# A long convolution by transforms beside a sliding-window attention: the second transform level moved to 64x64 tiles

## The chip, the cores and the metric

The kernel runs on one core of a Trainium2 chip. A core has a matrix engine (TensorE, PE in the profile, with PEld for its weight loads), three engines for elementwise work (VectorE or DVE, ScalarE or ACT, GpSimd or POOL), an engine that mostly issues transfers (SyncE or SP) and 16 DMA engines. PE writes into PSUM; DVE or ACT copies the results from there into SBUF (an eviction). The metric is the device time of one execution in microseconds.

## What is computed

Two independent parts, whose results stand side by side in the output rows (2048 rows of 576 + 576 bf16 numbers).

```
# A: attention over 8 positions, 2 apart, 32 heads of 18
q, k, v = split(x @ wqkv)                 # x: 2048 x 576
logits  = q[s] . k[s - 2*w] * 18**-0.5    # w = 0..7, masked below 0
o       = softmax(logits) . v[s - 2*w]
a       = o @ wo                          # 576 x 576

# B: short convolution, gate, long convolution, gate
k_shift = sum over t < 4 of k[s - t] * shift_k[:, t]
kv      = k_shift * v
y       = causal convolution of kv with ssm_k (2048 taps per channel)   # by rfft of length 4096
b       = q * (y + kv * ssm_D)
```

## The kernel before

**The long convolution** is done by a transform in two levels, in bf16 matmuls. Time is split as s = 16a + t, with a on the 128 partitions and t = 0..15. The first level (`s1_part`; steps `sx` for the signal kv, `kp` for the taps, which `kt` transposes first) multiplies by a 128x128 table for the real and one for the imaginary part and gives, for each first frequency f of 128, 32 rows: 16 t by real and imaginary. The results go to scratch arrays in DRAM (`Dk`, `Dx`) with f and rows exchanged, so that the second level can have the rows on the partitions. There f is split as (l, h). Step `kl` or `xl` number i loads one block (`w_load`), step `ks` or `xs` transforms it (`k_spec`, `x_spec`, helper `s2`), `gp` multiplies the two spectra (`g_prod`), `gi` transforms back (`g_inv`) and writes to the scratch `Dy`. `yl` loads it turned back (`y_load`), `ys` does the inverse of the first level and multiplies by q (`y_step`), and the result leaves for DRAM. There are 8 blocks i, each step of the second level runs twice per block (.0 and .1).

Before, a block is one half of the 576 channels (i // 4) and 8 of the 32 values of h (i % 4); the 128 partitions hold 32 rows by 4 values of l. `s2` uses tables of 128x64 with zeros between different l, one for the real and one for the imaginary part, and two matmuls side by side fill a PSUM tile. X and K then have real and imaginary part in separate columns; `g_prod` makes all four products of them; `g_inv` adds them up in four matmuls per tile of 64 x 128, with a third table that is the negative of the first (`ia_minus`, steps `im`). A scratch row is 288 numbers, 576 bytes. A `yl` needs the four blocks of its own half of the channels.

**The attention**: `xt` transposes x, `qk`, `qt` and `v` project it, `lm` multiplies q by a shifted k on DVE, `lb` sums over heads on PE, `sm` is the softmax for one half hv of the positions, `pm` multiplies the weights with shifted v on DVE, `ps` sums over the window by identity matmuls on 64x64 tiles, `po` is the output projection (72 matmuls of 32x128 tiles, 288 columns), and `pz` is a `po` with the last two `ps` inside. `po.0.*` needs all nine `ps.0.*`.

**The order.** One list, `ORDER`, written out by hand or by a planner outside the kernel, gives all steps. Each engine runs its own instructions in this order, and the order holds for the queues of SP (almost all transfers) and POOL (the Dy writes and a small halo of v) as well; semaphores make an instruction wait for data or for a free buffer, and all behind it on its engine wait too. A step may carry marks: `a` or `b` names one of two PSUM pools (two tiles each), `s` or `v` says that ACT or DVE does its eviction. Without a mark `evac` uses ACT (L102, DVE is L104), and the copies of `xt` and `kt` use DVE (L359). Buffers come from small rings: four slots for loaded blocks, two each for K, X and the products.

Of the kernel before, what the change touches and what calls it, by code (L numbers as in the profile page):

```python
# [18 lines left out]
lx.2.1 lx.2.0 lx.1.1 lx.1.0 tj lx.0.1 t0 lx.0.0 tv lwt t2 lwq.0.1 lwq.1.1 wm.11:b xt.2.2:bs xt.2.0:bs xt.1.0:as sk.2:b  # L19
xt.1.2:bs xt.1.1:as t3 xt.2.1:b sk.1:a xt.0.0:bs qk.0.1.1:a lx.3.0 lx.3.1 lk.1 tw sk.0:av qk.1.1.2:b xt.0.2:a xt.0.1:b  # L20
xt.3.1:a t4 lk.0 wt cv.0.0 cv.0.4 lkn.4 xt.3.0:as lkn.0 xt.3.2:bs qk.1.1.1:b lkn.1 qk.0.1.3:b cv.1.1 lkn.2 qt.1:b
cv.1.4 qt.3:a lkn.3 lwq.0.0 qt.2:b lv.0 cv.0.1 lk.2 lwq.1.0 lwv cv.1.0 kt.7:b kt.1:a cv.0.3 kp.7.0:a cv.0.2 cv.1.3
kp.7.1:b cv.0.5 cv.1.5 kp.7.2:b kt.2:as qk.0.0.0:a t5 lv.1 cv.0.6 kp.1.0:b cv.1.2 lk.3 kp.1.1:a cv.0.7 qk.1.0.2:b
kp.1.2:a cv.1.6 cv.1.7 kt.0:bs ib ia.5 kp.2.0:a qk.0.1.2:b ld cv.2.1 cv.2.4 kp.2.1:a kp.2.2:a qt.0:b lv.3 sx.0.0:b
qk.0.0.2:a sx.0.1:b cv.2.3 sx.0.2:a qk.0.0.1:b kp.0.0:a kp.0.1:a qk.0.0.3:b lv.2 ia.2 kp.0.2:a sx.1.0:b sx.1.1:a
qk.0.1.0:b sx.1.2:b qk.1.0.0:a t1 cv.3.3 cv.3.4 ia.3 cv.2.5 sx.2.0:b cv.3.1 sx.2.1:a cv.2.0 cv.2.2 cv.3.5 qk.1.1.3:b
cv.2.6 sx.2.2:av kt.3:a sx.3.0:b sx.3.1:bv kt.5:as sx.3.2:a cv.3.0 qk.1.1.0:b kp.3.0:a cv.3.2 kp.3.1:b qk.1.0.3:a
kp.3.2:a ia.7 cv.3.6 cv.2.7 kp.5.0:bv ia.1 kp.5.1:b kt.4:as kp.5.2:b kt.6:as ia.0 cv.3.7 qk.1.0.1:b lm.0.1 sx.4.0:a
sx.4.1:b sx.4.2:a v.4:b lm.0.2 v.0:b lm.6.2 lm.0.0 lb.0:a sx.6.0:a sx.6.1:b lm.6.0 sx.6.2:b lm.6.1 kp.4.0:a ia.4
lb.6:a kp.4.1:b kp.4.2:a ia.6 lm.7.0 v.8:b lm.7.1 sx.7.0:b sx.7.1:a sx.7.2:a lb.7:b sx.5.0:b sx.5.1:a sx.5.2:a lm.4.0  # L30
lm.1.0 v.7:b kp.6.0:a kp.6.1:b kp.6.2:a kl.3 lm.1.1 lm.4.2 lb.1:b xl.3 im.0 xl.2 xl.5 v.2:a lm.2.0 v.5:a im.1 lm.4.1
lm.2.2 lb.4:b v.1:b lm.2.1 lm.5.0 lb.2:b ks.3.0:a v.3:b vh.0 xs.3.0:a lm.5.1 xs.3.1:b lb.5:a kl.5 ks.3.1:b lm.3.0 kl.6
vz xs.5.0:a lm.3.1 lb.3:b xs.5.1:a vh.1 ks.5.0:b gp.3.0 sm.0.0 ks.5.1:a sm.1.0 ql.1 sm.0.1 ql.3 sm.1.1 sm.0.2 sm.0.3
sm.1.2 sm.0.4 kl.2 gp.3.1 sm.1.3 xs.2.0:bv v.6:a xl.6 sm.0.5:a lwo.3 gi.3.0:a lwo.0 sm.0.6 xs.2.1:a kl.0 gp.5.0 pm.0.1
vh.2 ks.6.0:b ks.6.1:a gi.5.0:b gp.5.1 gi.3.1:a ps.0.1:b xs.6.0:a xs.6.1:b ks.2.0:a pm.0.0 gp.6.0 pm.0.3 sm.1.4
ps.0.0:b xl.0 lwo.2 gi.5.1:a xl.1 sm.1.5:b pm.0.7 gp.2.0 gi.6.0:a gp.6.1 ks.2.1:b ps.0.3:a kl.1 sm.1.6 xs.0.0:b
gi.6.1:a pm.0.5 ps.0.7:b gp.2.1 pm.0.6 ks.0.0:a pm.1.0 ks.0.1:b xl.7 gi.2.0:a ps.0.5:b gi.2.1:a gp.0.0 xs.1.0:b
ks.1.0:a ps.0.6:b gp.1.0 xs.1.1:a gi.0.0:b xs.0.1:a ql.0 pm.1.3 ps.1.0:b ks.1.1:a kl.7 ps.1.3:b gp.0.1 ql.2 xs.7.0:a
pm.0.8 gi.1.0:b gp.1.1 kl.4 xl.4 gi.0.1:a pm.0.4 ks.7.0:b gi.1.1:a ps.0.8:b ks.4.0:b lwo.1 ks.4.1:a pm.0.2 xs.4.0:b
# [9 lines left out]
def kernel(  # L49
# [50 lines left out]
    def evac(dst, src, scale=None, on="s"):  # L100
# [8 lines left out]
    Dx = dram.tile([2, 32, 128, HD], BF16, name="Dx")  # L109
    Dy = dram.tile([2, 32, 128, HD], BF16, name="Dy")  # L110
    VT = 528

    def by_f1(Dd, dh, r0, n):
        return Dd[dh].rearrange("r f d -> f r d")[:, r0:r0 + n, :]
# [105 lines left out]
    mk = r2  # L220
# [484 lines left out]
```

## Time and profile before

Three runs took 208.24, 208.3 and 210.26 us, median 208.3. The profiled execution took 208.09 us; its span, from first to last instruction of the program, is 206.1 us, so 2 us lie around it. TensorE's granted clock was 1.0 until the last slices (0.995 in the mean).

| stretch (us) | what runs | PE | DVE | ACT | DMA share |
|---|---|---|---|---|---|
| 0 to 20 | loads, tables, transposes of x | 17.0 of 20 | 15.7 | 14.1 | 0.95 |
| 20 to 60 | first level, projections, short convolution | 39.4 of 40 | 37.5 | 34.2 | 0.86 |
| 60 to 105 | first level, logits | 43.7 of 45 | 44.7 | 37.5 | 0.68 |
| 105 to 120 | second level begins, softmax | 13.2 of 15 | 14.2 | 14.1 | 0.94 |
| 120 to 169.5 | second level, weights times v | 46.0 of 49.5 | 48.3 | 48.9 | 0.87 |
| 169.5 to 201.3 | output projection, last inverse level | 31.2 of 31.8 | 21.0 | 14.2 | 0.93 |
| 201.3 to the end | last evictions and writes | 0 of 4.8 | 0 | 1.2 | 0.60 |

Busy times are those of the engine in that stretch. PE's come from pipelined matmuls, so a full PE need not be at its peak. DMA moved 51.5 MB in 54,398 packets, most of them of 576 bytes.

### The profile page before, as it was taken

What the parts mean: (1) busy time and instruction counts of PE and PEld (TensorE: products, weight loads), DVE (VectorE), ACT (ScalarE), POOL (GpSimd) and SP (SyncE); (2) the same over time, 40 slices, a digit from 0 to 9 for tenths busy, and PEclk for the clock granted to TensorE, in tenths of its full rate; (3) what the DMA queues carried; (4) which work ended last, traced back from release to release, by engine and by line L of the source; (5) the groups of instructions that cost most, each with busy time, mean ns of one, the idle gap of its engine ahead of it and who ended that gap; (6) DMA issues with size and microseconds to landing.
All of it is one profiled execution on the core that took longest, in us unless ns stands there. A gap on an engine that the chain in (4) does not pass through costs nothing.

```text
span 206.1 us, 6334 instructions
## 1 busy us (share of the span) xinstructions
PE 190.5 (92%) x2725; PEld 123.7 (60%) x2725; DVE 181.3 (88%) x160; ACT 164.1 (80%) x251; POOL 13.0 (6%) x39
## 2 busy tenths in 40 slices
PE   7699999999999999999998798899998999999990
PEld 2456465444465674556655575666666669876880
DVE  7877999997899999999999999999999989871740
ACT  2698788997879968897598999999999984804342
POOL 8300000000000000000210101111011011000000
PEclk9999999999999999999999999999999999999997
DMA  6999999789743874966958999987498598899995
GB/s 170 310 384 231 405 343 267 241 258 257 212 130 115 227 198 132 195 189 157 413 140 271 275 205 305 256 321 276 144 368 283 175 329 305 214 318 280 266 257 176
DMA packets 54398, 51.50 MB, mean 250 GB/s; under 512 B 6769, under 2 KB 48354, under 8 KB 54370
## 3 DMA queue, kind: packets, MB, share of 16 engines
q1 hardware_dynamic: 53120, 46.32, 77.1%
q0 software_dynamic: 1248, 4.77, 6.2%
q8 instruction: 21, 0.34, 0.7%
q14 instruction: 7, 0.06, 0.1%
q10 hardware_dynamic: 2, 0.00, 0.0%
HBM read 31.04 MB, written 18.87 MB: 242 GB/s over the span
## 4 chain that ended last, share of the span: by engine, by line
PE 56%; ACT 31%; issue 5%; DMA 2%; POOL 2%; DVE 2%; ACTq 1%; SPq 0%; DVEq 0%; POOLq 0%
ACT area L102 28%; PE psB L373 11%; PE psA L612 7%; PE psA L373 5%; PE psB L380 4%; PE psA L652 3%; PE psA L428 2%; PE psA L601 2%; DMA Dk<-area 2%; PE psB L612 2%; PE psA L380 2%; ACT area L528 2%; PE psB L428 2%; PE psB L601 2%; PE psB L578 2%
## 5 line engine op out<-in xcount | busy, mean ns | idle before, releaser
L102 ACT ACTIVATE area<-psA 128x576 bf16<-128x576 f32 (+6 forms) x119 | 86.5, 782 | 19.6 <-PE psB L612 9.1
L102 ACT ACTIVATE area<-psB 128x576 bf16<-128x576 f32 (+8 forms) x118 | 83.9, 749 | 12.4 <-PE psB L373 4.9
L590 DVE TENSOR_TENSOR area<-area,area 128x4096 bf16<-128x4096 bf16 x18 | 40.7, 2283 | 0.0
L489 DVE TENSOR_TENSOR area<-area 128x4096 bf16<-128x4096 bf16 x16 | 35.7, 2285 | 0.3 <-PE psB L506 0.2
L373 PEld LDWEIGHTS <-area 128*128 128x128 bf16 x160 | 15.5, 98 | 17.1 <-issue 0.4
L373 PE MATMUL psB<-area,area 128*128 128x512 bf16 x110 | 25.4, 379 | 0.1
L457 DVE TENSOR_TENSOR area<-area,area 128x2304 bf16<-128x2304 bf16 x16 | 21.0, 1351 | 2.6 <-PE psB L428 1.9
L565 DVE TENSOR_TENSOR area<-area 128x2304 bf16<-128x2304 bf16 x16 | 21.6, 1353 | 1.2 <-ACT area L102 1.1
L543 PEld LDWEIGHTS <-W 128*64 128x64 bf16 x256 | 13.7, 108 | 11.3 <-issue 11.0
L612 PE MATMUL psA<-area,area 32*128 32x288 bf16 x288 | 19.4, 282 | 0.6 <-ACT area L102 0.3
L612 PE MATMUL psB<-area,area 32*128 32x288 bf16 x288 | 19.2, 282 | 0.0
L380 PEld LDWEIGHTS <-area 128*32 128x32 bf16 x360 | 15.6, 140 | 4.7 <-issue 1.4
L612 PEld LDWEIGHTS <-area 32*128 32x128 bf16 x576 | 16.1, 93 | 3.6 <-issue 1.6
L601 PEld LDWEIGHTS <-ident 64*64 64x64 bf16 x576 | 15.1, 107 | 3.5 <-issue 2.8
L578 PEld LDWEIGHTS <-IAt 64*128 64x128 bf16 x256 | 12.4, 94 | 6.4 <-issue 3.3
L451 DVE TENSOR_TENSOR area<-area,area 128x2304 bf16<-128x2304 bf16 x12 | 15.8, 1352 | 0.1
L543 PE MATMUL psA<-area,W 128*64 128x288 bf16 x136 | 13.3, 291 | 1.3 <-ACT area L102 0.3
L428 PEld LDWEIGHTS <-T 128*128 128x128 bf16 x96 | 8.7, 98 | 9.4 <-issue 2.8
L380 PE MATMUL psB<-area,area 128*32 128x512 bf16 x240 | 14.1, 382 | 0.2 <-ACT area L102 0.2
L428 PE MATMUL psA<-area,T 128*128 128x384 bf16 x54 | 13.1, 327 | 0.6 <-ACT area L102 0.4
L601 PE MATMUL psB<-area,ident 64*64 64x256 bf16 x384 | 12.6, 271 | 0.2
L543 PE MATMUL psB<-area,W 128*64 128x288 bf16 x120 | 11.4, 290 | 1.3 <-ACT area L102 0.9
(112 smaller groups left out, 212.2 us busy)
## 6 DMA issues: line engine op xcount, KB each, us to landing
Dk<-area SPq DMA_DIRECT2D x16, 288.0 KB, 3.5
Dx<-area SPq DMA_DIRECT2D x16, 288.0 KB, 3.0
area<-Dk SPq DMA_DIRECT2D x8, 576.0 KB, 4.9
area<-Dx SPq DMA_DIRECT2D x8, 576.0 KB, 6.7
Dy<-area POOLq DMA_DIRECT2D x8, 576.0 KB, 4.4
area<-Dy SPq DMA_DIRECT2D x8, 576.0 KB, 5.2
area<-in_A_wo_dram SPq DMA_DIRECT2D x4, 648.0 KB, 9.4
area<-in_A_x_dram SPq DMA_DIRECT2D x8, 288.0 KB, 5.5
```

The source lines that it names most:

```text
L102: nc.scalar.activation(dst, src, ACT.Copy, **({} if scale is None else {"scale": scale}))
L373: nc.tensor.matmul(ps[:, u, :], w[:, kb, cols[u]:cols[u] + 128], xT[:, j, kb], start=(kb == 0), stop=(kb == 4))
L380: nc.tensor.matmul(ps[32 * a:32 * a + 32, u, :], wv[:, kb, 2 * n + u:D:DH], xT[:, a, kb], start=(kb == 0), stop=(kb == 4), tile_position=( ...
L428: nc.tensor.matmul(ps[:, ri, 0:384], T1[:, ri, :], sf[:, 384 * ch:384 * ch + 384], start=True, stop=not extra)
L457: nc.vector.tensor_tensor(dst, kfull[:, 4 * c + 3 - j:4 * c + 7 - j, :], skb[:, j, :].unsqueeze(1).to_broadcast([128, 4, D]), ALU.mult)
L489: nc.vector.tensor_tensor(prr.get((n, h)), q2[h], k2[h][:, :, o0:o0 + S], ALU.mult)
L543: nc.tensor.matmul(ps[64 * hp:64 * hp + 64, im, 0:HD], W2[:, im, 8 * g + 2 * prl + hp].rearrange("p l f -> p (l f)"), Wt[:, 2 * prl + hp, ...
L565: nc.vector.tensor_tensor(Pv, Xv.unsqueeze(2).to_broadcast([128, 2, 2, 2 * HD]), Kv.unsqueeze(1).to_broadcast([128, 2, 2, 2 * HD]), ALU.mult)
L578: nc.tensor.matmul(ps[:, hp, 0:HD], IAt[r, tab, 4 * g + 2 * hv + u, :], Pp[(i, hv)][r, n, u, :], start=(n == 0), stop=(n == 3), tile_posit ...
L590: nc.vector.tensor_tensor(Pr.get((hv, p)), vv, Lt[:, :, 256 * hv:256 * hv + 256].unsqueeze(2).to_broadcast([128, W, 2, 256]), ALU.mult)
L601: nc.tensor.matmul(ps[64 * b:64 * b + 64, r, 0:256], ident[g, g], P[g, n, :, 128 * b:128 * b + 128], start=(n == 0), stop=(n == W - 1), ti ...
L612: nc.tensor.matmul(pss[e][:, b, 0:HD], Os[hv][g, d // 2, r, 128 * (d % 2):128 * (d % 2) + 128], wo4[g, d, d0:d1], start=(d == 0), stop=(d ...
```

## The change

The second level works on 64x64 tiles. A block is now 4 of the 32 values of h and all 576 channels; the partitions hold two halves a of f, each 32 rows by 2 values of l. Four matmuls of 64x64 fill a PSUM tile, one in each quarter of the array, and real and imaginary part lie on neighbouring partitions of the result. For the product each partition needs its own part of K and its neighbour's, so a new step `kz` (`k_swap`) copies K with odd and even partitions exchanged, by two transfers from SBUF to SBUF. `gp` makes the two products, `gi` adds them up in two rounds of four 64x64 matmuls instead of four rounds of two. The table for `gi` comes from a new array `Wp`, which the new step `tp` (`t_pairs`, three ACT copies) fills; `im` goes. Scratch rows are 576 numbers, 1152 bytes, so are the rows of q and of the output, except for half of the attention's. A `yl` now needs all eight blocks. One memset moves from `tv` to `ld`. K's ring gets an area of its own.

The list of steps is written anew from the first to the last: the order, the PSUM pools and the evicting engines are all different. The first convolution is now `cv.0.1` instead of `cv.0.0`; the blocks of the second level come as 3 5 1 4 7 0 2 6 instead of 3 5 6 2 0 1 7 4; two of the five `kt` copies that ACT made are now DVE's; the inverse first level `ys` starts behind the first four `po`, where two steps of it ran ahead of the first `po`.

```diff
-    Dk = dram.tile([2, 32, 128, HD], BF16, name="Dk")
+    Dk = dram.tile([2, 32, 64, D], BF16, name="Dk")
...
     def t_w2():
         nc.scalar.preload_act_table_set("natural_log_exp_and_others")
-        for i in range(2):
-            nc.vector.tensor_tensor(W2[:, i], C2[:, 32 * i:32 * i + 32].unsqueeze(2).to_broadcast([128, 32, 4, 16]),
-                                    lmask.unsqueeze(1).to_broadcast([128, 32, 4, 16]), ALU.mult)
+        nc.vector.tensor_tensor(W2.rearrange("p h (l f) -> p h l f", l=2), C2.unsqueeze(2).to_broadcast([128, 32, 2, 32]),
+                                lmask.unsqueeze(1).to_broadcast([128, 32, 2, 32]), ALU.mult)
+
+    def t_pairs(i):
+        dst = Wp[:, i].rearrange("p h (f j) -> p (h f) j", j=2)
+        src = W2[:].rearrange("p h (f i) -> p (h f) i", i=2)[:, :, i:i + 1]
+        if i:
+            evac(dst, src.to_broadcast([128, 1024, 2]))
+        else:
+            evac(dst[:, :, 0:1], src)
+            evac(dst[:, :, 1:2], src, scale=-1.0)
...
-    def s2(Wt, g, dst, h, scale):
-        for prl in (2 * h, 2 * h + 1):
+    def s2(Wt, i, dst, q, scale):
+        for d0, d1 in DCH:
             ps = psb()
-            for im in range(2):
-                for hp in range(2):
-                    nc.tensor.matmul(ps[64 * hp:64 * hp + 64, im, 0:HD],
-                                     W2[:, im, 8 * g + 2 * prl + hp].rearrange("p l f -> p (l f)"),
-                                     Wt[:, 2 * prl + hp, :], start=True, stop=True, tile_position=(0, 64 * hp))
-            evac(dst[:, :, prl, :], ps[:, :, 0:HD], scale=scale)
+            for e in range(2):
+                for a in range(2):
+                    r = slice(64 * a, 64 * a + 64)
+                    nc.tensor.matmul(ps[64 * e:64 * e + 64, a, 0:HD], W2[r, 4 * i + 2 * q + e], Wt[r, 2 * q + e, d0:d1],
+                                     start=True, stop=True, tile_position=(64 * a, 64 * e))
+            evac(dst[:, q, :, d0:d1], ps[:, :, 0:HD], scale=scale)
...
+    def k_swap(i):
+        for e in range(2):
+            nc.sync.dma_start(Kr[i][e:128:2, 1], Kr[i][1 - e:128:2, 0])
...
-    def g_inv(i, hv):
-        dh, g = i // 4, i % 4
-        Y = Yr[i] if hv else Yr.get(i)
-        for u in range(2):
+    def g_inv(i, q):
+        Y = Yr[i] if q else Yr.get(i)
+        for d0, d1 in DCH:
             ps = psb()
-            for n, tab in enumerate((0, 1, 1, 2)):
-                for hp in range(2):
-                    r = slice(64 * hp, 64 * hp + 64)
-                    nc.tensor.matmul(ps[:, hp, 0:HD], IAt[r, tab, 4 * g + 2 * hv + u, :], Pp[(i, hv)][r, n, u, :],
-                                     start=(n == 0), stop=(n == 3), tile_position=(64 * hp, 0))
-            evac(Y[:, 4 * hv + 2 * u:4 * hv + 2 * u + 2, :], ps[:, :, 0:HD])
+            for n in range(2):
+                for e in range(2):
+                    for a in range(2):
+                        r = slice(64 * e, 64 * e + 64)
+                        nc.tensor.matmul(ps[64 * a:64 * a + 64, e, 0:HD], IAt[r, n, 2 * i + q, 64 * a:64 * a + 64],
+                                         Pp[(i, q)][r, n, a, d0:d1], start=(n == 0), stop=(n == 1), tile_position=(64 * e, 64 * a))
+            evac(Y[:, 2 * q:2 * q + 2, d0:d1], ps[:, :, 0:HD])
...
-    def y_load(i):
-        dh, c4 = i // 4, i % 4
-        nc.sync.dma_start(Wr.get(("y", i)), by_f1(Dy, dh, 8 * c4, 8))
+    def y_load(c2):
+        slot = Wr.get(("y", c2))
+        for a in range(2):
+            nc.sync.dma_start(slot[64 * a:64 * a + 64], by_f1(Dy, a, c2))
```

Of the new list, the stretch where the second level ends (marks as above):

```diff
+xs.6.1:a lwo.1 ps.0.7:b ps.0.1:b gp.6.0 gi.2.1:a gp.6.1 gi.6.0:a pm.1.1 gi.6.1:b ql.0 ql.5 yl.2 yl.0 ps.1.1:av yl.5
+po.0.1.0 po.0.0.0 yl.4 pm.1.5 pm.1.8 po.0.1.1 po.0.0.1 ys.2.0:b ys.2.1:as ps.1.5:av pm.1.7 ql.6 yl.3 ys.5.0:as
```

More of the change, by code (lines that the diff above doesn't have):

```diff
@@ L24 @@
[L24 to L28, printed above, removed]
@@ L263, in load_D @@
     def load_D():
+        nc.vector.memset(knats[4][64:128, :], 0.0)
         nc.sync.dma_start(Db[0:1, :], B_ssm_D.unsqueeze(0))
@@ L617, in p_fin @@
         for e in range(2):
-            stage = sAr.get((hv, r, di, e))
-            evac(stage, pss[e][:, :, 0:HD])
+            key = (hv, r, e) if hv == 0 else (hv, r, di, e)
+            stage = sAr[key] if hv == 0 and di else sAr.get(key)
+            evac(stage[:, :, d0:d1], pss[e][:, :, 0:HD])
             a = 4 * (2 * r + e) + 2 * hv
-            nc.sync.dma_start(outt[:, a:a + 2, d0:d1], stage)
-            sAr.drop((hv, r, di, e))
+            if hv:
+                nc.sync.dma_start(outt[:, a:a + 2, d0:d1], stage[:, :, d0:d1])
+            elif di:
+                nc.sync.dma_start(outt[:, a:a + 2, 0:D], stage)
+            if hv or di:
+                sAr.drop(key)
     def p_out(hv, r, di):
```

197 lines of the change are left out of this document (96 added, 101 removed).

## The prediction

> **What bounds the kernel now.** I read the page's busy shares first, then the engines by stretches of time, then who waited for whom, then the chain of work that ended last. The busy shares, from the page:
>
> ```profile
> ## 1 busy us (share of the span) xinstructions
> PE 190.5 (92%) x2725; PEld 123.7 (60%) x2725; DVE 181.3 (88%) x160; ACT 164.1 (80%) x251; POOL 13.0 (6%) x39
> ```
>
> They point at PE, and PE is what the change relieves. A busy PE counts pipelined matmuls, so the same shares by stretch (us; columns PE, PEld, DVE, ACT, POOL busy, clock, DMA share, GB/s) say more:
>
> ```profile
> 20.00:60.00 40.00, 39.42 (x235) 20.90 (x234) 37.45 (x32) 34.16 (x46) 0.00 (x0) 1.00 0.86 268
> 60.00:105.00 45.00, 43.65 (x574) 27.06 (x576) 44.66 (x25) 37.48 (x50) 1.86 (x3) 1.00 0.68 196
> 120.00:169.50 49.50, 46.04 (x832) 32.22 (x831) 48.28 (x28) 48.87 (x90) 3.80 (x7) 1.00 0.87 266
> 169.50:201.30 31.80, 31.16 (x793) 25.36 (x792) 21.02 (x27) 14.18 (x25) 0.53 (x1) 1.00 0.93 274
> ```
>
> Up to 105 us PE and DVE are both full. From 120 to 169.5, where the second transform level runs, ACT works 48.9 and DVE 48.3 of 49.5 us; PE is the one with room. From 169.5 PE alone is full: the output projections. The waits of DVE from 15 to 169.5 us:
>
> ```profile
> DVE area L457 <- PE psB L428: 1.9, 1, 1.9
> DVE area L565 <- ACT area L102: 1.1, 2, 0.9
> ```
>
> From its first convolution at 18.46 to the end of its last spectral product at 167.51 DVE stands idle about 4.5 us in all. The last product, gp.4.1, waited for ACT:
>
> ```profile
> 166.15 1.36 DVE L565 TENSOR_TENSOR area<-area 128x2304 bf16<-128x2304 bf16 x1 [0.95 <-ACT area L102]
> ```
>
> The chain of work of 120 to 169.5 us, by line, agrees; ACT's evictions are 60% of it, the matmuls of ks, xs (L543) and gi (L578) 18%:
>
> ```profile
> by line: ACT area L102 60.1%; PE psB L578 7.4%; issue 6.3%; PE psA L601 6.1%; PE psA L543 4.9%; ACT area L528 4.2%; PE psB L543 3.9%; PE psA L652 2.4%; PE psA L578 2.2%; PE psB L601 2.0%; ACT area L533 0.6%; ACTq L102 0.2%; ACT area L534 0.
> ```
>
> **PE's saving.** ks and xs make 64 PSUM groups of four matmuls of 288 columns; two run beside each other today, four after. A pair costs about 0.12 us: the 72 output matmuls of one po step, four abreast, stream from 169.54 to about 171.9, 18 waves of 0.13. A group falls from 0.24 to 0.12, 64 x 0.12 = 7.7 us. gi has 32 groups of eight half-height matmuls, four waves today, two after: 32 x 0.24 = 7.7. PE streams 15.4 us less. That four 64x64 quarters run together is seen in ps (L601): 32 matmuls of 256 columns in 1.0 us is eight waves.
>
> **What doesn't fall.** ks, xs and gi still make 32 + 32 + 32 evictions of 128x576 (0.53 us apart on ACT from 131.5 on), and the products stay 16 of 128x2304 at 1.35 us. So in the stage that binds nothing of this saving reaches ACT or DVE, and I cost it at nothing; were PE the bound there, it would be worth up to 15.4 us.
>
> **DVE's work ahead of its last product** decides, so I count it from the first convolution, in the two orders. Before: 13 pm steps ahead of gp.4.1. After: 14 ahead of gp.6.1, one more of 2.28 us. Key transposes copied by DVE: three, then five, 2 x 0.75 = 1.5. xs.2.0 no longer evicts on DVE: minus 2 x 0.75. First-level evictions on DVE: three in both. Sum **+2.3 us**. One table product of 1.22 us goes (L339), the memset of 0.91 moves to ld, and t_second fuses small ones: all before the convolutions, where DVE waits for loads, worth nothing. tp adds three ACT copies, about 4.2 us (1024 elements 1.09, 2048 elements 2.0, the nearest rows), im takes away two of 1.09: 2 us more ACT work before 60 us, where ACT has 5.8 us of room; if not, that is the cost.
>
> **Start.** SP issues are in order. Before lk.0 has landed, both orders move about 4.6 MB (x, four or two wqkv parts, and k). In the old order cv.0.0 needs only the body of lk.0 and runs at 18.46; cv.0.4 waits till 20.46. In the new one the first is cv.0.1, which needs the halo too, so about 20.2 for everything. One product of 1.35 us is not done by then: **+1.2 us** (0 to 1.4).
>
> **The wait that goes.** When DVE reaches the end of cv.3.7, PE has 6 us of work less in front of it in the new list, so the stall of 1.9 us at 52 should go: **-1.9 us** (0 to -3.5 with the rest of the idle time).
>
> **The exchange.** kz adds 16 SP transfers of 288 KB from SBUF to SBUF. No row shows one. Nearest: Dx writes of the same 288 KB landing in 3.0 us, loads of 576 KB in 4.9 and 6.7. From the second ks eviction: 1.1 of ACT, 0.8 of SP issues, 3.0 to 6.7 to land, 4.9 to 8.6 us. On DVE wait gp.i.0 and everything behind it, pm and gp, then gi, ps. The DVE work that the list has between ks.i.1 and gp.i.0 is, in order of time, 9.1, 12.2, 4.5, 9.4, 8.2, 7.2, 3.6 and 5.9 us. At 4.9 it is short by 0.4 and 1.3; at 8.6 by 4.1, 0.4, 1.4, 5.0 and 2.7, nearly 14. Today DVE starts a product 2.6 us (median) after its inputs were ready, which covers the first: I take the value near the row of equal size, **+0.5 us**, and keep 0 to 14. kz also stands in SP's queue ahead of kl and xl loads; those are four slots deep.
>
> **DMA.** By the trace's packet records 576 bytes take 29 ns, 1152 take 51, 4608 take 178. About 34,800 small rows become half as many: 63.1 - 55.5 = 7.6 us of 16 engines saved; the exchange adds 1024 x 178 / 16 = 11.4. No relief in all.
>
> **Tail.** Today y loads of one half of D wait for four gi groups, and ys.1 runs before the last gi. After, each y load needs all eight. From the end of gp.6.1: gi 0.4, evictions 1.1, Dy write 0.53 + 4.4, y load 0.5 + 5.2: 12.1 us. Ahead of ys.2 stand pm.1.1 and ps.1.1 (2.28 + 0.1 + 0.9) and four po of 2.4: 12.9. Hidden; without the four po, ys would wait 9 us. PE then has 29.7 us after its first po, against 30.4 today (eight po 2.4 each incl. pz, ys 0.49, ps 0.87). Today's tail from first po to the span's end is 36.6; po starts 2.0 us after gp.4.1, then 3.2 after gp.6.1. 3.2 + 29.7 + 6.2 = 39.1 against 38.6: **+0.5 us**. The y, q and output rows after it need some 31 us of DMA, about what it has today.
>
> **Sum.** 2.3 + 1.2 - 1.9 + 0.5 + 0.5 = +2.6 us. The profiled execution took 208.09 us (span 206.1 and 2 around it), 0.2 under the median of the three runs, 208.3; 208.1 + 2.6 gives **210.7 us**, so 208.5 to 213 with the small bounds.
>
> **Two rules weighed.** PE's weight loads before ks and xs stand idle on "issue":
>
> ```profile
> PEld L543 <- issue: 11.0, 38, 0.8
> ```
>
> The Trainium skill (TensorEngine Tiling (Array Packing), Key Properties) says that a change of tiling mode, not just of tile, drains TensorE. By that rule ks, gi and ps, which have three shapes today and one after, would lose part of these 11.0 us besides; the chain from 100 to 170 us has 4.9 us of such "issue", so it would make the first rival below up to 4.9 us faster still (198.3), and leave my sum, which is not PE's, where it is.
> The Trainium skill (DMA: Bandwidth & Descriptors, Rules for kernel authors) says that two transfers to disjoint partition halves serialize and should be one. By it an exchange of two interleaved halves costs what 576 KB cost, the upper end above: the second rival. That y loads are split in two would add SP issues of 0.4 us each, which no run has shown yet.
>
> **The rivals.**
> - **PE is on the path after all (faster), 0.20.** For it: PE 92%, and the chain from 100 to 170 us holds 9.7 us of L543 and L578 matmuls. Half of that goes: 208.1 - 4.9 = 203.2. Against it: ACT's 48.9 of 49.5. It decides if DVE's and ACT's idle time in the second level falls below today's 2 us and the list starts the tail earlier.
> - **The exchange holds DVE (slower), 0.22.** 6.7 us landings while DMA is 0.87 full; half of 14 us: 210.7 + 7 = 217. It decides from a landing of about 4.5 us.
> - **DVE's idle time goes and it starts at 18.5 (no change), 0.08.** 210.7 - 2.7 = 208.0.
> - **The quarters don't overlap, 0.02.** Each group then takes four or eight waves: PE's second level needs some 15 us more than today, 220. L601 speaks against it.
> - My forecast holds 0.48.
>
> **How the numbers follow.** One per cent, 2.1 us, is about what a measurement of this kernel can tell from no change: 206.2 to 210.4. The forecast's spread lies 0.18 within and 0.30 above; with the others: faster 0.20, within 1% 0.26, slower 0.54. Range: 204 leaves half of the first rival out below, 217 half of the second above: 204 to 217.
>
> **What would show it.** Right: L543 and L578 busy less by about half, PE's share near 85%, ACT and DVE still over 97% in the second level, the last L565 ending near 169.5, the first po about 3 us behind it. Exchange: L565 waiting for a DMA of area from area. Start: the first L457 at about 20. Wrong: if the last L565 ends before 167, or if the time from it to the end is not about 39 us, the count above has missed what sets it.

## The result: 229.9 us, and the profile after

The changed kernel takes **229.86 us** (median of four runs, 227.34 to 231.54) against 208.27 for the kernel before, run beside it: a ratio of **1.092, 95% interval 1.080 to 1.104**. The forecast was 210.7, the range 204 to 217. The direction was right, the size was far off. Here and below a time is the median of all runs while a ratio compares the faster runs of each kernel alone (227.34 and 228.37 here), and the profiled execution, 231.35 us (span 229.3), was one of two in a slower state, so up to 3.5 us of what its profile shows belong to that state.

The busy shares, from the page of the changed kernel:

```profile
PE 184.5 (80%) x2718; PEld 117.4 (51%) x2725; DVE 178.3 (78%) x156; ACT 169.4 (74%) x255; POOL 12.8 (6%) x39
```

PE's busy time fell by 6 us while the span grew by 23. DVE is busy 3 us less and ACT 5 us more than before; both simply stand idle for longer. The stretches say where (us; then length; PE, PEld, DVE, ACT, POOL busy with counts; granted clock, DMA share, GB/s). The last two lines cut the span at the last spectral product, which now ends at 178.0:

```profile
20.00:60.00 40.00, 36.60 (x194) 18.15 (x197) 35.92 (x30) 32.43 (x41) 0.00 (x0) 0.96 0.83 223
60.00:105.00 45.00, 41.59 (x492) 24.51 (x495) 42.44 (x28) 38.24 (x54) 1.25 (x2) 1.00 0.77 201
120.00:178.00 58.00, 41.02 (x883) 30.40 (x881) 53.31 (x33) 54.19 (x95) 4.01 (x7) 0.85 0.84 269
...
19.54:178.03 158.49, 133.63 (x1814) 81.94 (x1817) 146.31 (x101) 136.71 (x207) 6.01 (x10) 0.94 0.84 243
178.03:229.30 51.27, 34.26 (x792) 26.17 (x784) 18.33 (x22) 19.62 (x33) 1.07 (x2) 0.93 0.83 233
```

The same two stretches of the kernel before, first convolution product to last spectral product, and from there to the end:

```profile
18.46:167.51 149.05, 141.85 (x1794) 88.30 (x1793) 143.90 (x101) 134.03 (x207) 5.99 (x10) 1.00 0.82 243
167.51:206.10 38.59, 33.15 (x816) 26.47 (x813) 23.01 (x28) 17.08 (x29) 1.06 (x2) 0.97 0.89 263
```

The 23.2 us by which the span of the profiled execution grew are 10.5 ahead of the last product and 12.7 behind it. Ahead: the first product starts 1.1 us later, DVE has 146.31 - 143.90 = 2.4 us more work, and its idle time goes from 149.05 - 143.90 = 5.2 to 158.49 - 146.31 = 12.2 us: 1.1 + 2.4 + 7.0 = 10.5. Behind: PE has 34.3 us of work, 1.1 more than before, but waits for 17 us where it waited for 5.4.

What DVE waited for ahead of the last product (engine, line, released by what; us in total, times, longest):

```profile
DVE area L596 <- PE psB L607: 3.7, 2, 2.8
DVE area L368 <- PE psA L479: 2.2, 3, 0.8
DVE area L368 <- PE psB L479: 2.1, 1, 2.1
DVE area L459 <- DMA area<-in_B_k_dram: 0.8, 1, 0.8
```

Before, the only such row above 1.1 us was one wait of 1.9. Now DVE waits for PE in several places: the products of weights and v (pm, L596), whose buffer a sum (ps, L607) still reads, and the copies of the transposed taps (kt; the copy is L368, the transpose L479).

And behind the last product (DVE's waits from 178 us on, then two rows of other engines):

```profile
DVE area L666 <- issue: 8.8, 1, 8.8
DVE area L666 <- ACT area L102: 7.6, 4, 5.3
DVE area L666 <- PE psB L662: 6.8, 1, 6.8
...
ACT area L102 <- DMA Dy<-area: 2.1, 1, 2.1
...
SPq L651 <- DMA Dy<-area: 15.3, 1, 15.3
```

L666 is the output product (ys). DVE stands idle ahead of it three times: for the first y block (6.8), in the middle (5.3), and before ys.3.0 (8.8). The 8.8 us have no releaser in the profile, but ys.3.0 starts at 216.65, just behind the landing of its q load at 216.57, which was issued only at 208.6. In gi_twice (below), whose list of steps is the same, the three stalls are 6.6, 5.8 and 5.5 us: the places recur, the sizes are those of one execution. The transfers, from the page (KB each, median us from issue to landing):

```profile
area<-area SPq DMA_DIRECT2D x16, 288.0 KB, 3.0
Dy<-area POOLq DMA_DIRECT2D x8, 576.0 KB, 5.3
area<-Dy SPq DMA_DIRECT2D x16, 288.0 KB, 7.6
out_dram<-area SPq DMA_DIRECT2D x12, 288.0 KB, 7.5
```

The exchange (area from area) lands in 3.0 us. The y loads of half the former size land in 7.6 by the median, where the former ones of 576 KB took 5.2. The chain of work that ended last runs through them (start, us, what; three of its pieces):

```profile
172.05 7.74 DMA Dy<-area
...
191.54 8.10 DMA area<-Dy
199.66 7.38 DMA area<-Dy
```

### The profile page after: what moved, and what is told of

It reads as the page before. It is cut to its first block, busy times and chain, and to the rows that moved or that the text cites. A ratio compares the mean times of both kernels' runs of the same rounds, so it can differ in the third digit from the quotient of the medians.

```text
span 229.3 us, 6371 instructions
## 1 busy us (share of the span) xinstructions
PE 184.5 (80%) x2718; PEld 117.4 (51%) x2725; DVE 178.3 (78%) x156; ACT 169.4 (74%) x255; POOL 12.8 (6%) x39
## 4 chain that ended last, share of the span: by engine, by line
PE 22%; ACT 16%; DMA 14%; issue 12%; SPq 1%; DVE 1%; POOL 0%; ACTq 0%; DVEq 0%; POOLq 0%
ACT area L102 14%; DMA area<-Dy 7%; PE psA L618 4%; PE psB L389 4%; DMA Dy<-area 3%; DMA area<-Dk 2%; PE psB L618 2%; DMA Dk<-area 2%; ACT area L530 2%; PE psA L662 1%; PE psB L534 1%; SPq L651 1%; PE psB L508 1%; PE psA L389 1%; PE psB L382 1%
## 5 line engine op out<-in xcount | busy, mean ns | idle before, releaser
L102 ACT ACTIVATE area<-psA 128x576 bf16<-128x576 f32 (+6 forms) x117 | 82.2, 744 | 38.9 <-PE psA L662 11.6
L102 ACT ACTIVATE area<-psB 128x576 bf16<-128x576 f32 (+6 forms) x123 | 85.0, 729 | 13.2 <-PE psB L389 4.4
L596 DVE TENSOR_TENSOR area<-area,area 128x4096 bf16<-128x4096 bf16 x18 | 40.6, 2285 | 3.7 <-PE psB L607 3.7
L459 DVE TENSOR_TENSOR area<-area,area 128x2304 bf16<-128x2304 bf16 x16 | 21.0, 1353 | 1.3 <-DMA area<-in_B_k_dram 0.8
L607 PEld LDWEIGHTS <-ident 64*64 64x64 bf16 x576 | 18.7, 120 | 5.6 <-issue 3.1
L382 PE MATMUL psB<-area,area 128*128 128x512 bf16 x88 | 20.6, 379 | 0.4 <-ACT area L102 0.2
L618 PE MATMUL psA<-area,area 32*128 32x288 bf16 x288 | 19.5, 288 | 0.3 <-ACT area L102 0.3
L546 PEld LDWEIGHTS <-W 64*64 64x64 bf16 x256 | 9.3, 112 | 20.0 <-issue 19.1
L618 PE MATMUL psB<-area,area 32*128 32x288 bf16 x288 | 19.4, 288 | 0.0
L389 PEld LDWEIGHTS <-area 128*32 128x32 bf16 x360 | 15.4, 140 | 5.4 <-issue 2.1
L618 PEld LDWEIGHTS <-area 32*128 32x128 bf16 x576 | 16.1, 95 | 3.6 <-issue 1.1
L382 PE MATMUL psA<-area,area 128*128 128x512 bf16 x65 | 17.5, 406 | 0.4 <-issue 0.2
L546 PE MATMUL psA<-area,W 64*64 64x288 bf16 x144 | 10.9, 324 | 6.3 <-ACT area L102 6.0
L430 PEld LDWEIGHTS <-T 128*128 128x128 bf16 x96 | 8.7, 98 | 11.4 <-issue 6.2
L662 PEld LDWEIGHTS <-IB 128*128 128x128 bf16 x64 | 6.3, 104 | 14.2 <-issue 12.3
L662 PE MATMUL psA<-area,IB 128*128 128x288 bf16 x36 | 6.8, 319 | 7.4 <-DVE area L666 3.5
L430 PE MATMUL psA<-area,T 128*128 128x384 bf16 x52 | 12.2, 326 | 0.5 <-ACT area L102 0.5
L546 PE MATMUL psB<-area,W 64*64 64x288 bf16 x112 | 8.3, 314 | 5.1 <-ACT area L102 4.5
```

Of the source, the lines that this page charges most:

```text
L102: nc.scalar.activation(dst, src, ACT.Copy, **({} if scale is None else {"scale": scale}))
L382: nc.tensor.matmul(ps[:, u, :], w[:, kb, cols[u]:cols[u] + 128], xT[:, j, kb], start=(kb == 0), stop=(kb == 4))
L389: nc.tensor.matmul(ps[32 * a:32 * a + 32, u, :], wv[:, kb, 2 * n + u:D:DH], xT[:, a, kb], start=(kb == 0), stop=(kb == 4), tile_position=( ...
L430: nc.tensor.matmul(ps[:, ri, 0:384], T1[:, ri, :], sf[:, 384 * ch:384 * ch + 384], start=True, stop=not extra)
L459: nc.vector.tensor_tensor(dst, kfull[:, 4 * c + 3 - j:4 * c + 7 - j, :], skb[:, j, :].unsqueeze(1).to_broadcast([128, 4, D]), ALU.mult)
L546: nc.tensor.matmul(ps[64 * e:64 * e + 64, a, 0:HD], W2[r, 4 * i + 2 * q + e], Wt[r, 2 * q + e, d0:d1], start=True, stop=True, tile_positio ...
```

## The experiments

For each run the ratio is that to the kernel before on the same chip, with its 95% interval. The table cuts each profiled span in the same way; "idle" is DVE's between its first convolution product and its last spectral product.

| run | us, ratio [95%] | last product ends | from there to the end | DVE idle ahead |
|---|---|---|---|---|
| before | 208.3 | 167.5 | 38.6 | 5.2 |
| after | 229.9, 1.092 [1.080, 1.104] | 178.0 | 51.3 | 12.2 |
| old_code_new_order | 220.5, 1.056 [1.043, 1.069] | 173.3 | 44.3 | 8.3 |
| no_exchange | 225.5, 1.079 [1.069, 1.089] | 176.4 | 47.8 | 10.8 |
| half_y_loads | 224.1, 1.073 [1.067, 1.080] | 177.3 | 45.3 | 11.4 |
| pz_early | 232.0, 1.101 [1.092, 1.111] | 174.2 | 53.5 | 8.4 |
| gi_twice | 229.3, 1.097 [1.087, 1.107] | 179.8 | 48.9 | 14.1 |
| three_wo | 221.1, 1.061 [1.054, 1.068] | 176.8 | 42.1 | 10.6 |

Up to the last product, half_y_loads and pz_early are the changed kernel itself: their edits come into effect behind it. Yet DVE stands idle there for 11.4 and 8.4 us, against 12.2. Single executions of one program differ by some 4 us in this column, so smaller differences in it settle nothing.

### The order or the code

**old_code_new_order**: the transforms, layouts and transfers of before, run in the order of the new list.

```diff
-ORDER: the old list
+ORDER: the new list without tp.0, tp.1 and kz.0 to kz.7; im.0 and im.1 stand where kz.3 and kz.5 stood
```

> The code of the kernel before with the new list of steps, without tp and kz, with the two im where kz.3 and kz.5 stood. Theory 1, the new list costs: 222 us or more. Theory 2, the new code costs: 208 to 213 us.

Measured: 220.52, 1.056, between the two expectations and nearer to the first. By these values **over half of the loss is the new list** (5.6 of 9.2 points: its order, PSUM pools and evicting engines), with not one instruction of the new transform in it. Its profile by the two stretches:

```profile
18.64:173.30 154.66, 141.48 (x1822) 86.46 (x1821) 146.40 (x101) 135.41 (x207) 6.30 (x11) 1.00 0.77 221
...
173.35:217.60 44.25, 32.66 (x786) 25.20 (x783) 18.00 (x22) 19.23 (x33) 0.70 (x2) 0.95 0.94 269
```

DVE does the 146.4 us of work of the new kernel: the 2.4 us more (one pm more ahead of the last product, two more copies of transposed taps) are the list's. To this come 3.1 us of idle time and 5.7 us behind the last product. There the first ys stands at 188.1 us, 14.8 after the last product, though an old y load needs only four of the eight blocks: in the new list they all stand behind the last gi. In the kernel before, four of eight are issued at 160.7 to 165.2 and the first ys runs as the products end.

**new_code_old_order**: the converse. The new code in the old list, with the least that its dependences ask for.

```diff
-ORDER: the new list
+ORDER: the old list; tp.0, tp.1 behind cv.0.4, each kz right behind its second ks, im left out;
+       three second ks moved up; yl.0 to yl.3 and ys.1 moved behind the last gi
-        nc.vector.memset(knats[4][64:128, :], 0.0)
+        nc.vector.memset(knats[4][64:128, :], 0.0)
```

> The changed kernel's code with the list of steps of the kernel before. tp is put in behind the first convolutions, kz right behind the second ks of each block (three second ks steps move up beside the first, so that kz stands ahead of gp), the four early y loads and ys.1 move behind the last gi, since a y load now needs all eight blocks; the memset of the key rows goes back to tv. Theory 1, the new list is what costs: 208 to 213 us, the last spectral product ends near 168 to 171. Theory 2, the new code costs (the exchange, and y loads that all stand behind the last block): 220 us or more, with a tail behind the last product near 50 us as in the changed kernel.

Measured: 250.40, 1.201 [1.192, 1.210]. The old order is far worse for the new code. Here the exchange does hold DVE:

```profile
DVE area L666 <- ACT area L102: 20.3, 4, 11.6
DVE area L571 <- DMA area<-area: 15.6, 4, 4.8
```

A product (L571) waits four times for the transferred half, up to 4.8 us, because the old list has a product soon after its ks. The new list puts other DVE work there.

**first_new** and **second_new**: the old code, with the new list up to the first block load and the old list from there, and the other way round. **new_code_old_first**: the new code with the old first part.

```diff
 first_new:          ORDER: new list up to kl.3, then the steps left over, in the old order
 second_new:         ORDER: old list up to kl.3, then the steps left over, in the new order
 new_code_old_first: as second_new, with the new code
```

> The code of the kernel before; the list is the new one up to the first load of a block (kl.3, about 90 us), and then the old order of all steps not yet done. The old code with the whole new list took 12.6 us more than before (220.5). If the first half of the new list costs: 213 us or more. If the second half does: 206 to 210.

> The code of the kernel before; the old list up to the first load of a block (lm.4.0 left to its new place, or its buffer ring is too short), and then the new order of the rest. If the second half of the new list costs (blocks in the new order, all y loads behind the last gi, four po ahead of the first ys): 216 to 221 us. If the first half does: 208 to 212.

> The changed code with the old list up to the first load of a block (tp put in behind the first convolutions) and the new list for the rest. If the first half of the new list costs part of the changed kernel's loss: 222 or less. If not: 226 to 230.

Measured: 217.78 (1.041 [1.036, 1.047]), 227.69 (1.088 [1.083, 1.094]) and 239.64 (1.143 [1.136, 1.149]). The last two lie above all that was expected of them. The two halves of the list, alone, cost 4.1% and 8.8%, together 5.6%. They don't add. Each splice has a stall that the whole list has not, which would account for it, though no run shows that it does; the largest of first_new:

```profile
DVE area L489 <- PE psB L506: 6.3, 2, 5.7
```

and of second_new:

```profile
DVE area L493 <- PE psA L498: 4.7, 1, 4.7
DVE area L489 <- PE psA L506: 2.0, 1, 2.0
```

So the order's loss ahead of the last product could not be pinned to one half. Its end could: from the last product to the end first_new takes 38.2 us, as before (38.6), and second_new 45.0. The longer end comes from the second part of the list.

### The exchange

**no_exchange**:

```diff
-    kz.0 ... kz.7 in ORDER
-        Kv = Kr[i][:, :, q].rearrange("p n a d -> p n (a d)")
+        Kv = Kr[i][:, 0, q].rearrange("p a d -> p (a d)").unsqueeze(1).to_broadcast([128, 2, 2 * D])
```

> The changed kernel without kz; the product takes the same copy of K for both of its halves, so y comes out wrong, everything else is the same work. Theory 2 in the form that the exchange holds VectorE or the transfers behind it: 7 us or more faster than the changed kernel (222 or less). Theory 1: 227 to 230, since the changed kernel's VectorE shows no wait for a DMA of area from area.

Measured: 225.48, 1.079 [1.069, 1.089]. That is 1.3 points, some 2.7 us, below the changed kernel; the intervals overlap, so 2.7 is the best value and no settled price. DVE's idle time falls by 1.4 us, less than executions of one program differ by, and the end by 3.5. The work of the DMA engines falls clearly: by the pages' queue shares they are busy for 84.5% of 229.3 us with the exchange and 79.3% of 224.2 without, 194 and 178 us. In the changed kernel no product waits for the exchange. In three of the runs below products did (y_from_dx, half_y_loads and q_early, up to 2.1, 0.5 and 2.3 us at a time); the longest:

```profile
DVE area L572 <- DMA area<-area: 2.3, 1, 2.3
```

### PE's saving, and its clock

**matmuls_twice**: ks, xs and gi issue each matmul twice, which gives back the PE time that the change saves.

```diff
+                    for _ in range(2):
-                    nc.tensor.matmul(ps[64 * e:64 * e + 64, a, 0:HD], W2[r, 4 * i + 2 * q + e], Wt[r, 2 * q + e, d0:d1],
-                                     start=True, stop=True, tile_position=(64 * a, 64 * e))
+                        nc.tensor.matmul(ps[64 * e:64 * e + 64, a, 0:HD], W2[r, 4 * i + 2 * q + e], Wt[r, 2 * q + e, d0:d1],
+                                         start=True, stop=True, tile_position=(64 * a, 64 * e))
...
-            for n in range(2):
+            for n in (0, 1, 0, 1):
```

> The changed kernel with every matmul of ks, xs and gi issued twice with the same result, so TensorE streams the 15.4 us again that the 64x64 tiles saved. Clock theory (the saving leaves TensorE idle enough that its granted clock falls to a half four times between 28 and 170 us, and slow matmuls then hold the other engines): no slower than the changed kernel, 221 to 228 us, the clock at 1.0 up to the tail. If TensorE's saving is worth anything by itself: slower than the changed kernel, 232 or more. The kernel before with the new list, whose TensorE does the old work, showed no fall of the clock.

Measured: 233.02, 1.114 [1.106, 1.123]: with the saving given back the kernel is 2.3 points slower, some 4.7 us, and the intervals lie just apart (1.104 and 1.106). So on this list the saving is worth something, as the second expectation had it, but far less than the 15.4 us that were counted as streamed. This run showed something else too: its clock is full up to 179 us, while that of the changed kernel is halved four times ahead of the last product. The changed kernel around two of these places (columns as above, the clock third from the end):

```profile
148.20:151.60 3.40, 1.81 (x41) 1.18 (x44) 3.40 (x3) 3.40 (x7) 0.00 (x0) 1.00 1.00 339
151.60:155.00 3.40, 3.40 (x64) 2.95 (x56) 3.40 (x3) 2.71 (x6) 0.53 (x1) 0.50 0.68 272
124.30:127.70 3.40, 1.72 (x39) 1.11 (x40) 3.40 (x3) 3.40 (x7) 0.00 (x0) 1.00 0.99 201
127.70:131.10 3.40, 1.67 (x28) 0.70 (x16) 3.40 (x3) 3.40 (x5) 0.00 (x0) 0.50 0.49 184
```

In these two places a step of 3.4 us in which PE is busy for half is followed by one at half clock. In the first pair PE is then busy for all of it. The largest wait of DVE ahead of the last product, 2.8 us for a ps, ends at 169.0, behind a stretch at half clock from 161.8 to 168.6. So a second theory was that PE, relieved, loses its clock, and that this makes the 7 us of idle time.

**gi_twice** tests it: only gi is doubled, half of the saving given back.

```diff
-            for n in range(2):
+            for n in (0, 1, 0, 1):
```

> The new kernel with the matmuls of the inverse second level (gi) issued twice, 7.7 us of TensorE work given back; ks and xs are as in the new kernel. Theory, halved clock: the clock stays full between 120 and 175 us, DVE's idle time from the first convolution product to the last spectral product falls from 12.2 us to 8 or 9, the last product ends near 174.5, and the time is 226. Rival, the clock is a sign and no cause: the idle time stays at 11 to 14 us and the time is 229 to 232.

Measured: 229.27, 1.097 [1.087, 1.107]. From the first convolution product to the last spectral one:

```profile
19.24:179.78 160.54, 133.79 (x2052) 83.80 (x2059) 146.47 (x101) 136.95 (x208) 6.40 (x11) 1.00 0.83 242
```

The clock is full throughout and DVE's idle time is 160.54 - 146.47 = 14.1 us, not less. The wait for ps is down to 0.7 us, but the products now wait for gi:

```profile
DVE area L571 <- PE psA L584: 3.1, 1, 3.1
DVE area L571 <- ACT area L102: 1.5, 1, 1.5
DVE area L571 <- PE psB L584: 1.2, 1, 1.2
```

**The theory of the clock falls** as an account of the loss: the clock moves the waits, but a kernel with a full clock up to its last product is no faster. That filling PE loses in work what it gains in clock would fit this; no run of the new code has the full clock without the extra work, so the two are not separated.

### Behind the last product

**y_from_dx**: the y loads read another scratch array (Dx) of the same shape, so they don't wait for the writes of Dy; y is then computed from Dx, without the second level's result.

```diff
-            nc.sync.dma_start(slot[64 * a:64 * a + 64], by_f1(Dy, a, c2))
+            nc.sync.dma_start(slot[64 * a:64 * a + 64], by_f1(Dx, a, c2))
```

> The changed kernel, but the y loads read Dx, which is complete long before, in place of Dy: same bytes and rows, no wait for the last block's write; y comes out wrong. If the wait for the last block (SyncE waits 15.3 us for Dy in the changed kernel) sets the tail: 219 to 223. If the queue of transfers behind it does (y, q and output rows at 1.07 of the DMA engines, 7.6 us to land): 226 to 229.

Measured: 226.16, 1.082 [1.072, 1.092]; 49.6 us from the last product to the end. The wait of SP for Dy (15.3 us in the changed kernel) is gone, its first loads go out from 169.9 us on, and yet the first ys stands at 195.8. The chain before it goes through PE: 46% of the stretch from 176 to 200 us is po (L618), after one write of Dy that ACT's eviction of gi.6.0 waits for, and which takes 9.4 us with the early y loads beside it, where it took 7.7 (start, us, what):

```profile
169.49 9.38 DMA Dy<-area
```

PE works in the order of the list, in which four po stand ahead of the first ys, and they start late since the last gi does. In the changed kernel the four po end some 2 us before the first y block has landed (192.8 us), so to cure the wait of the loads alone can gain little more than that.

**half_y_loads**: four of the eight pairs of y loads are left out.

```diff
-        for a in range(2):
+        for a in range(2 if c2 in (2, 0, 5, 4) else 0):
```

> The changed kernel with four of the eight y loads left out; the four y blocks concerned use what the slot held, so half of y is wrong. 2.3 MB less behind the last product. If the amount of transfers sets the tail (from 190 to 220 us the DMA engines are full): 219 to 223. If single waits do (a late instruction in a queue): 226 to 229.

Measured: 224.12, 1.073 [1.067, 1.080]; 45.3 us to the end. It lies between the two expectations, and is the largest gain of any single cure, about 1.8 points, 4 us: the amount of transfers is part of the end's price.

**pz_early**: pm.1.7, ps.1.5 and pz stand ahead of the first ys, which in DVE's order held them back.

```diff
-... po.0.0.1 ys.2.0 ys.2.1 ps.1.5 pm.1.7 ql.6 yl.3 ... yl.1 pz.1.0.0 ys.4.0 ...
+... po.0.0.1 pm.1.7 ps.1.5 pz.1.0.0 ys.2.0 ys.2.1 ql.6 yl.3 ... yl.1 ys.4.0 ...
```

> The changed kernel with pm.1.7, ps.1.5 and pz.1.0.0 moved ahead of ys.2.0 in the list. In the changed kernel pm.1.7 stands behind ys.2.0 on VectorE, which waits 6.8 us for the first y load, and pz waits for pm.1.7. If this order of VectorE's queue costs: 3 to 6 us faster (222 to 225). If the transfers set the tail: 227 to 230.

Measured: 231.97, 1.101 [1.092, 1.111]: nothing gained. The idle time ahead of ys.3.0 is 10.4 us here, against 8.8: its q load comes late all the same.

**q_early**: four more buffers for q (over a free K buffer), and all q loads issued by the end of gp.2.1.

```diff
+    qx = [Kr.slots[0][:, n, q] for n in range(2) for q in range(2)]
-    qtr = Ring(*[mk.take(2, D) for _ in range(4)])
+    qtr = Ring(*[mk.take(2, D) for _ in range(4)], *qx)
     ORDER: ql.0 ql.5 ahead of kl.6; ql.6 ql.3 ql.1 ql.7 behind gp.2.1
```

> The changed kernel with four more slots for q, laid over the first slot of K, so that all q loads are issued by the end of gp.2.1 and none in the tail (in the changed kernel ys.3 waits 8.8 us, its q load issued at 208.6). If single late loads cost: 3 to 7 us faster (221 to 225). If only the amount of transfers counts: about 5 us faster too, since 1.8 MB leave the tail; no gain at all would say that neither does.

Measured: 226.43 (222.05 to 229.32) against 209.04 for the kernel before beside it, so 1.083; its runs spread too far for an interval. In its profile the stall of 8.8 us ahead of ys.3.0 is gone and the one of 5.3 at ys.4.0 stays; one of 4.3 at ys.6.0 is new, the first ys waits 8.5 us instead of 6.8, and the end takes 46.7 us.

**three_at_once**: no exchange, half the y loads, and q early.

```diff
 the edits of no_exchange, half_y_loads and q_early together
```

> The changed kernel without the exchange, with half of the y loads and with the q loads early, all three as in the single runs; y is partly wrong. The single runs gained about 3, 4.5 and 3 us. If these are separate costs: 217 to 220 us. If they are the same waits seen three times: 222 to 225.

Measured: 224.94, 1.077 [1.069, 1.084]: no more than one of them alone. The profile names what came in their place. A piece of its chain (start, us, what):

```profile
174.81 8.10 DMA area<-in_A_wo_dram
```

and PE's longest wait between 170 and 190 us, ahead of the first output projection:

```profile
PE psB L619 <- DMA area<-in_A_wo_dram: 3.0, 1, 3.0
```

The last part of wo (lwo.1) is issued at 174.8, behind three q loads that now stand ahead of it in SP's queue; in the changed kernel it went out at 168.2. It lands at 182.9 and the first ys slips to 197.3. One late load was cured by making another late. The single run of q_early has the same late load of wo (issued at 174.7).

**three_wo, q_wo, four_wo**: lwo.1 ahead of the later q loads, in three_at_once and in q_early; four_wo also puts pm.1.7 and ps.1.5 ahead of the first ys.

```diff
-... gp.2.1 ql.6 ql.3 ql.1 ql.7 gi.2.0 xs.6.0 xs.6.1 lwo.1 ...
+... gp.2.1 lwo.1 ql.6 ql.3 ql.1 ql.7 gi.2.0 xs.6.0 xs.6.1 ...
 four_wo: -po.0.1.1 po.0.0.1 ys.2.0 ys.2.1 ps.1.5 pm.1.7
          +pm.1.7 ps.1.5 po.0.1.1 po.0.0.1 ys.2.0 ys.2.1
```

> The new kernel without the exchange (K's own copy stands for the other half), with four of the eight y loads left out (the unloaded blocks keep old data) and with the q loads early, as in the run of the three cures at once, and the load of the last quarter of wo issued ahead of the later q loads. Theory, late loads: the first output projection starts within 2 us of the last gi eviction instead of waiting till 183 us for wo, from the last product to the end it takes about 43 us instead of 47.6, and the time is 220 (against 224.9 for the three cures alone). Rival, the stretch is bound by TensorE's and the DMA engines' throughput: 224 to 226.

> The new kernel with the q loads early and the last quarter of wo ahead of the later q loads; nothing is left out. Theory, late loads: 2 to 3 us less than with the early q loads alone (226.4), so about 224. Rival: 226 to 227, since the y loads decide.

> The run three_wo with the product pm.1.7 and the sum ps.1.5 moved ahead of the first output product ys.2.0 on DVE; the same parts are left out. Theory, in-order queue: the zero-th row's output (pz) no longer follows ys.2.0, the end comes 2 us earlier than in three_wo, 218. Rival: the same as three_wo within 1 us, as moving them gave nothing in the full kernel.

Measured: three_wo 221.07 (1.061 [1.054, 1.068]), q_wo 226.28 (1.085 [1.077, 1.093]), four_wo 220.78 (1.057 [1.050, 1.063]). three_wo is as the theory of late loads had it: 1.6 points below three_at_once, and the end is 42.1 us:

```profile
176.81:218.90 42.09, 33.08 (x792) 24.75 (x784) 18.28 (x23) 19.30 (x33) 1.07 (x2) 0.93 0.70 212
```

q_wo went by its rival: with all y loads in place no gain shows over q_early, whose runs spread by 7 us. So the load of wo counts in three_wo and not here; three_wo leaves out both the exchange and half of the y loads, and which of them covers it was not tested. four_wo, too, went by its rival; the order of pm.1.7 on DVE is not what is late. In sum: with the exchange gone, half of the y loads gone and the other loads early, the new code takes what the old code takes on the same list (1.061 and 1.056, intervals overlapping). **Most of the 3.6 points that the new code adds to its list goes when transfers are left out and late loads are moved.** How much of it is lateness is not shown: half of the y loads are work that the kernel must do, and the old code on the new list, with all of its own y loads, was not given the early loads. No version of the new code beat the kernel before.

## Why the prediction was wrong in size

Step by step, as the prediction put it.

- **PE's saving is worth nothing: too low, by a few microseconds.** Given back in full it costs 4.7 us, just clear of the intervals; given back by half, 1.1 us, well inside them. The reason given (DVE and ACT are full, PE is not) held in the kernel before; in the new one DVE waits for PE. The first rival (PE on the path, faster) did not come: the saving did not show as a gain. The saving itself was counted too large: L543 and L578 were busy 24.7 and 19.2 us and were to lose 15.4 (or, by the list of signs, about half, 22); their successors are busy 19.2 and 13.6, a loss of 11.2:

```profile
L546 PE MATMUL psA<-area,W 64*64 64x288 bf16 x144 | 10.9, 324 | 6.3 <-ACT area L102 6.0
L546 PE MATMUL psB<-area,W 64*64 64x288 bf16 x112 | 8.3, 314 | 5.1 <-ACT area L102 4.5 <-DMA area<-Dk 0.3
L584 PE MATMUL psB<-area,IAt 64*64 64x288 bf16 x160 | 9.0, 322 | 2.4 <-ACT area L102 2.2
L584 PE MATMUL psA<-area,IAt 64*64 64x288 bf16 x96 | 4.6, 285 | 1.7 <-ACT area L102 1.6
```

  Part of it is the half clock: a matmul of L546 takes 324 and 314 ns here and 292 and 294 in gi_twice, whose clock stays full in that stage. PE's share is 80%, forecast 85.
- **DVE's work ahead of its last product, +2.3: right.** It measured +2.4, and it is the list's.
- **Start, +1.2: right.** The first product (L459) starts at 19.5, 1.1 later.
- **The stall that goes, -1.9: wrong, the first failed step.** DVE's idle time was to fall and rose by 7.0 us. The prediction took it that a list with 6 us of PE work less ahead of one stall has fewer stalls; it looked at one stall and not at the new ones. That one stall did go (0.4 us is left of it). Of the 7.0 us the old code on the new list has 3.1 (in a single execution), and so has pz_early (8.4 - 5.2 = 3.2), which up to the last product is the changed kernel itself. The other 3.9, waits for PE by their rows (ps, transposed taps), come and go between executions, and their cause stays open.
- **The exchange, +0.5 (0 to 14): the low end was right for DVE.** The transfers landed in 3.0 us, the size of the nearest row, and no product waited in the changed kernel. Its price of some 2.7 us must then lie elsewhere; no run shows where. What the runs show beside it are 16 us of DMA work (194 against 178) and SP's queue, where each of the 16 transfers takes 0.59 us to issue. Both were named, and neither was summed. The second rival (the exchange holds DVE) is what happens in the old order: 15.6 us there, against the 14 that the prediction had as its upper end. The Trainium skill (DMA: Bandwidth & Descriptors, Rules for kernel authors) has two transfers to disjoint partition halves serialize. The two of a block, from the first issue to the second landing, took 3.1 to 4.9 us in five of the eight blocks, no more than a 576 KB load of K before (4.9), and 7.1 to 8.7 in the other three, which fell into stretches of full DMA (a share of 1.02 from 105 to 120 us and 1.03 around 172). So no cost of the rule is seen in the five, and the three don't settle it.
- **DMA, no relief: right in sign, too small.** 11.4 - 7.6 = 3.8 us more were summed. By the pages' queue shares the 16 engines were busy for 84.1% of 206.1 us before and for 84.5% of 229.3 after, 173 and 194 us: 20 more. 16 of them go with the exchange, and the longer rows save nothing that shows: it is 178 us in no_exchange and 178 in old_code_new_order, the old code on the same list. The sum took a packet of 1152 bytes at 51 ns, the median; by the packet records of the changed kernel's trace their mean is 67.
- **Tail, +0.5: the step that failed most.** It measured +12.7 in the profiled execution, and 48.9 - 38.6 = 10.3 in gi_twice, which has the same list. The prediction added PE's work and one latency: 12.1 us from gp.6.1 to the first ys, hidden behind 12.9 us of other work. Measured: 15.6. The 3.5 us more arise ahead of the last Dy write: ACT's eviction of gi.6.0 waits 2.1 us for a y buffer whose Dy write lands in 7.7, so the last Dy write is issued at 182.5, where the sum has it at 179.5. From there it went about as added: the write landed in 4.1 us, the first two y loads in 3.8 and 5.2. The larger part comes after, where the sum has no waits at all: the y loads issued from 189.6 on land in 7.0 to 8.6 us with DMA full, the q load of ys.3.0 is issued only at 208.6, and DVE waits 5.3 and 8.8 us more. It took "some 31 us of DMA, about what it has today" as cover. By the shares of the two stretches (0.83 of 51.3 us, 0.89 of 38.6) it is some 43 us of DMA, against 34 before: loads that were spread over the second level (four y loads at 160 to 165) now come behind it at once. The old code shows 5.7 us of the longer end from the list alone; that transfers are a part of the rest is shown by half_y_loads (an end of 45.3 us, against 51.3, and 48.9 in gi_twice), and the split of the rest stays open.
- **The check that was set:** "if the time from it to the end is not about 39 us, the count above has missed what sets it". It is 51.3, and the last product ends at 178.0 instead of near 169.5, with DVE and ACT at 92 and 93% in the second level instead of over 97%.
- **The rule on tiling modes.** The Trainium skill (TensorEngine Tiling (Array Packing), Key Properties) has a change of tiling mode drain TensorE. With ks, xs, gi and ps all on one mode the idle time of weight loads should have shrunk from 11.0 us. It grew, so no gain by that rule is seen. The row counts any idle time without a known releaser, though, and shrinks to 13.0 us in matmuls_twice, where PE has more to do, so it doesn't refute the rule either:

```profile
PEld L546 <- issue: 19.1, 32, 2.0
```

## What to carry to other kernels

An order written by hand for one version is part of that version: price it by running the old code in the new order and the new code in the old one before pricing any instruction. Where loads move behind the last product, count the end as a queue of transfers (issue time, landing at the load it will have, what stands ahead in each in-order queue), not as engine work plus one latency. A single late load can be hidden by other transfers: the early load of wo, which showed no gain with all transfers in place, was worth 4 us with half of the y loads and the exchange gone. And before a difference of a few microseconds in one row is explained, look at the same row in another execution of the same steps.

## What was not expected of the hardware

**The granted clock falls while PE works, not only when it stands still.** I cut all eighteen profiled executions into the 3.4 us steps in which the clock changes. In seventeen of them no drop from full clock followed a step in which PE was busy for more than 0.53 of the time; drops followed steps with 0.53, 0.51, 0.48 and less, though some steps of 0.41 to 0.53 stayed at full clock. In new_code_old_order two drops followed steps with 0.68 and 0.61, so 0.53 is no sharp limit. The clock came back only after steps with 0.82 and more. In the changed kernel the longest gap in PE's work in the four steps ahead of the drops before 170 us was 1.8 us. The Trainium skill (TensorE: Matmul & The Clock Gate, HAM oscillation) gives as its rule that PE should have no idle gaps above some 3.4 us; here gaps of at most 1.8 us were enough where they came to about half of the step. The kernel before, with PE at 92%, lost its clock only after 204 us.

**Transfers of half the size took longer:** 7.6 us for 288 KB against 5.2 for 576 KB by the median, both read from the scratch array Dy, the first with the profile's DMA share at 1.07 to 1.09 between 190 and 220 us. It is not the size: the first two of the 288 KB loads, issued at 186.8 and 187.6 us when the share was 0.37 (183.8 to 187.2) and 0.65 (187.2 to 190.6), landed in 3.8 and 5.2 us, those from 189.6 on in 7.0 to 8.6.
